# Sums in another form, casts and a table load behind the output's cast, and more output buffers, in a fused attention and mixture-of-experts kernel

## The chip, the cores and the metric

The kernel runs on one core of a Trainium2 chip. The metric is the device time of one execution in microseconds; before the change it is 619.33 us, the median of three runs (619.21 to 619.78). Five engines of the core work side by side: PE (TensorE, matrix products), DVE (VectorE), ACT (ScalarE), POOL (GpSimd) and SP (SyncE, which issues DMAs). Each runs its own queue of instructions in order and waits for others by semaphores.

## The reference

For 4 batches and 8 heads, with 576 positions of 64 numbers each, the attention computes

```python
scores = scale * q @ k.T          # causal mask
a = exp(scores - max); a /= a.sum(-1) + 1e-09
local = a @ v
q_p = phi(q)                      # x + 1 for x > 0, else exp(x)
mem_out = (q_p @ M_prev) / (q_p @ z_prev + 1e-06)
g = sigmoid(beta)                 # one number a head
attn = g * mem_out + (1 - g) * local
```

and its output, 2304 tokens of 512 numbers, goes through `(silu(x @ w_gate) * (x @ w_val)) @ w_out` with 1536 hidden units. All numbers are float32.

## The kernel before

The 32 heads are worked on as 16 pairs, `n` = 0 to 15. The loop over `n` (L543) is a pipeline of two pairs: iteration n computes the scores of pair n and the weighted values of pair n-1 (`old`), and splits the queries and keys of pair n+1; n=16 only drains. Products keep float32 precision by splitting each operand into a high and a low part (`qh`, `ql`, `kh`, `kl`, `xh`, `xl`) and adding three products.

For one pair: PE makes the scores tile by tile (`s`), DVE reads each from PSUM, masks it and takes the row's extreme (`mx`; the tiles `ps`, `pl` and, for the last 64 rows of both heads, `p`), ACT takes the exponential and the row's sum (`sm`), and POOL scales the row by the reciprocal of that sum, `rs`, times the gate `og` = 1 - g (function `weighed`, L436). `weighed` is called three times an iteration: for the four tiles of the first 256 rows, the four of the next 256, and the last 64 rows; the sum `sm + 1e-9` and its reciprocal stand on DVE, first with 128x4 numbers, again with 128x4, and then with 128x1. In an iteration of n=1 or more the first of these stands between `w` (the memory's normaliser) and `mem`, and behind `mem` come the readings of the next scores. The third stands right behind `ph`, DVE's part of phi, a `scalar_tensor_tensor` of 128x640 on two SBUF tiles. POOL's other work in an iteration is the splitting of pair n+1 (`kh`, `qh` early, `ql`, `kl` later).

PE transposes the scaled rows, ACT and DVE copy them to `g1` and `g2`, and PE multiplies them with the values into `tr`. `leave` (L517) casts this output: ACT makes `xh` (128x256 and then, at the next iteration's start, 128x320), DVE `xl`, and SP stores both to DRAM.

Four thirds of the experts' weights are decoded beside the attention (`EARLY`, n = 2, 6, 10, 14): the bits of two halves are put together by DVE (`wa`), and ACT casts the high part (`wgh`, `woh`) in `third_word` (L219), called at the end of n=5, 9 and 13. So the cast lies on ACT between the two `xh` casts. At n=16 ACT loads the table for Silu through a call on a 128x1 tile (`warm`, L553).

`gates` (L143) makes the gates once, in n=0. The order of instructions on PE, ACT, DVE and POOL is the order in the program: the helper `queued` (L79) ties each to the one before, and so nearly all rows carry L84. Exceptions are the DMAs and the cast of `kh` for pair 1, which a scheduler places. The second half of the kernel, from about 189 us on, is the mixture of experts; its output leaves through `away` (L782), with three `pt` buffers.

Of the kernel before, what the change touches and what calls it, by code (L numbers as in the profile page):

```python
# [9 lines left out]
F32 = mybir.dt.float32  # L10
# [3 lines left out]
AF = mybir.ActivationFunctionType  # L14
ALU = mybir.AluOpType
# [6 lines left out]
NP = B * NPAIR  # L22
# [7 lines left out]
ORDER = (0, 768, 1536)  # L30
EARLY, AHEAD = (2, 6, 10, 14), (1, 5, 9, 11, 12, 13, 14)
PLAIN = 3
ACT_K = (0, 1)
# [7 lines left out]
W_ONE = 2.0**-8  # L41
# [3 lines left out]
def attention_moe(ctx: ExitStack, tc: tile.TileContext, qt, kt_, v, m, beta, wg, wv, wo, out):  # L45
    nc = tc.nc
    PE, ACT, DVE, POOL, SP = nc.tensor, nc.scalar, nc.vector, nc.gpsimd, nc.sync

    const = ctx.enter_context(tc.tile_pool(name="const", bufs=1))
# [45 lines left out]
    def rot(pool, name, shape, dtype, n):  # L95
        held = slots.setdefault(name, [0, []])
        if len(held[1]) < n:
            held[1].append(pool.tile(shape, dtype, name=f"{name}{len(held[1])}"))
        held[0] += 1
        return held[1][(held[0] - 1) % n]  # L100
# [14 lines left out]
    warm = const.tile([128, 1], F32, name="warm")  # L115
# [18 lines left out]

    gt = const.tile([128, 8], F32, name="gt")
    gx = const.tile([128, NPAIR, 5, 2], F32, name="gx")

# [3 lines left out]
    def gates():  # L143
        act.activation(gs, gt, AF.Exp)
        act.activation(gt, gt, AF.Exp, scale=-1.0)
        gp, sp = (x.rearrange("p (r j) -> p r j", j=2) for x in (gt, gs))

        def one_less():
            dve.tensor_scalar(gs, gs, 1.0, None, op0=ALU.add)
            dve.reciprocal(gs, gs)  # L150
            dve.tensor_copy(og[:, :, 0:2], sp)
            for j in range(2):
                rows = slice(j * 64, j * 64 + 64)
                dve.tensor_copy(og[rows, :, 2], sp[rows, :, j])

        def memory():
            dve.tensor_scalar(gt, gt, 1.0, None, op0=ALU.add)
            dve.tensor_copy(gx, gp.unsqueeze(2).to_broadcast([128, NPAIR, 5, 2]))

        return one_less, memory  # L160
# [55 lines left out]
        else:  # L216
            act.activation(wa[n], last_byte, AF.Identity, scale=1.0 / 32, bias=low_bias)

    def third_word(act, dve, n):  # L219
        f, j = thirds[n]  # L220
        a, top = wa.pop(n), tops.pop(n).bitcast(I32)
        dve.scalar_tensor_tensor(
            out=a, in0=top, scalar=3, in1=a, op0=ALU.logical_shift_left, op1=ALU.bitwise_or
        )
        raws.pop(n)
        c = slice(j * 512, j * 512 + 512)
        if j < 2:
            SP.dma_start(wdr[f, :, c], a.bitcast(F32))
            if f >= PLAIN:
                return  # L230
            if j == 0:
                held[f] = [rot(wp, f"wg{part}", [128, 1024], F32R, 2) for part in "hl"]
            oh, ol = (x[:, c] for x in held[f])
        else:
            wout[f] = oh, ol = [rot(wp, f"wo{part}", [128, 512], F32R, 3) for part in "hl"]
        act.copy(oh, a.bitcast(F32))
        low_parts.append((f, j, a.bitcast(F32), oh, ol))

    def third(n):
# [9 lines left out]
    with tc.tile_pool(name="sb", bufs=1, reuse_waits="tile") as sb:  # L249
# [24 lines left out]
        def pair_split(n, raw):  # L274
            qr, kr = raw
            q = [rot(sb, f"q{part}", [128, 640], F32R, NK) for part in "hl"]
            k = [rot(sb, f"k{part}", [128, 576], F32R, NK) for part in "hl"]
            if n == 0:
                cuts = [(slice(0, 256), slice(0, 256)), (slice(256, 576), slice(256, 640))]
                lo = lambda dst, src, hi: dve.tensor_tensor(dst, src, hi.bitcast(F32), op=ALU.subtract)  # L280
                raw = qr[:, 128:768]
                for ck, cq in cuts:
                    act.copy(k[0][:, ck], kr[:, ck])
                    split_hi(q[0][:, cq], raw[:, cq])
                (ck, cq), (dk, dq) = cuts
                lo(k[1][:, ck], kr[:, ck], k[0][:, ck])
                lo(q[1][:, cq], raw[:, cq], q[0][:, cq])
                lo(k[1][:, dk], kr[:, dk], k[0][:, dk])
                return q, k, lambda: lo(q[1][:, dq], raw[:, dq], q[0][:, dq])
            (ACT.copy if n in ACT_K else split_hi)(k[0], kr)  # L290
            split_hi(q[0], qr[:, 128:768])

            def lows():
                split_lo(q[1], qr[:, 128:768], q[0], "q")
                split_lo(k[1], kr, k[0], "k")

            return q, k, lows
# [21 lines left out]
        class Pair:  # L319
# [58 lines left out]
            def scores(self, t):  # L378

                w = 128 * (t + 1)  # L380
                ps = [rot(psS, "s", [128, 512], F32, PS_S) for _ in range(2)]
                for i, (q, k) in enumerate(self.products):
                    for h in range(2):
                        rows = slice(h * 64, h * 64 + 64)
                        mm = pe.matmul(
                            ps[h][:, 0:w], q[rows, t * 128 : t * 128 + 128], k[rows, 0:w], start=(i == 0), stop=(i == 2)
                        )
                        if i == h == 0 and id(ps[1]) in read:
                            follow(mm, read[id(ps[1])], "once both banks are read", mybir.DependencyClass.Sync)

                def reading(h):
                    p = rot(sb, "pl", [128, 512], F32, NBIG) if t > 1 else rot(sb, "ps", [128, 256], F32, NSMALL)
                    read[id(ps[h])] = dve.tensor_tensor_reduce(
                        out=p[:, 0:w], in0=ps[h][:, 0:w], in1=maskp[:, 512 - w : 512], op0=ALU.add, op1=ALU.min,
                        scale=-SCALE, scalar=BIG, accum_out=self.mx[:, 2 * t + h : 2 * t + h + 1],
                    )
                    self.pts[(t, h)] = p

                return reading

            def exp(self, t, h):
                c, p = 2 * t + h, self.pts[(t, h)][:, 0 : 128 * (t + 1)]
                act.activation(
                    p, p, AF.Exp, bias=self.mx[:, c : c + 1], scale=-1.0, accum_out=self.sm[:, c : c + 1]
                )
# [27 lines left out]
                p = self.pts[(4, 0)][:, 0:576]  # L433
                act.activation(p, p, AF.Exp, bias=self.mx[:, 9:10], scale=-1.0, accum_out=self.sm[:, 8:9])

            def weighed(self, keys):  # L436

                c, n = keys[0][0] * 2, len(keys)
                rs = rot(sb, "rs", [128, 5], F32, 6)[:, 0:n]
                dve.tensor_scalar(rs, self.sm[:, c : c + n], 1.0e-9, None, op0=ALU.add)  # L440
                dve.reciprocal(rs, rs)
                for i, (t, h) in enumerate(keys):
                    p = self.pts[(t, h)][:, 0 : min(576, t * 128 + 128)]
                    g = h if t < 4 else 2
                    pool.tensor_scalar(
                        p, p, rs[:, i : i + 1], og[:, self.pr, g : g + 1], op0=ALU.mult, op1=ALU.mult
                    )

            def recalled(self):

# [89 lines left out]
        phi0 = pairs[0].phi_parts()  # L540
        nothing = lambda *args: None
        ending = lambda: nothing
        for n in range(NP + 1):  # L543
            cur = pairs[n] if n < NP else None
            old = pairs[n - 1] if n > 0 else None
# [3 lines left out]
            turned, turned1 = (old.turned, old.turned1) if old else (nothing, nothing)  # L549
            if cur:  # L550
                cur.begin()
            if n == NP:
                act.activation(warm, warm, AF.Silu)  # L553
            if old:
                old.turns()
            low = ending()
            reads = [scores(t) for t in range(2)]
            reads[0](0)
            reads[0](1)
# [15 lines left out]
            turned(2, 0, dve)  # L575
            turned(2, 1, dve)
            if n == NP:
                for i in range(2):
                    raw_top(act, len(EARLY) + i)
                third_clamp(pool, len(EARLY))  # L580
                third_move(pool, len(EARLY))
# [14 lines left out]
            reads = [scores(t) for t in range(2, 4)]  # L596
            reads[0](0)
            reads[0](1)
            exp(2, 0)
            exp(2, 1)  # L600
            turned(3, 0, act)
# [6 lines left out]
            exp(3, 1)  # L608
            if n == 0:
                one_less()  # L610
                first()
            read4()
            if cur:
                cur.exp4()
# [25 lines left out]
            for i, at in enumerate(EARLY):  # L640
                if n == at:
                    raw_top(act, i)
                if n == at + 1:
                    third_clamp(dve, i)
                if n == at + (2 if i < 3 else 1):
                    third_move(dve, i)
                if n == at + 3 and i < 3:
                    third_word(act, dve, i)
                if n == at + 4 and i < 3:
                    low_part(dve)  # L650
            if n in AHEAD:
# [10 lines left out]
    with tc.tile_pool(name="stg2", bufs=1, reuse_waits="tile") as stg2, \  # L662
# [117 lines left out]
                leave.append(lambda: away(t0, j))  # L780

        def away(t0, j):  # L782
            pt = rot(mbp, "pt", [128, 512], F32, 3)
            if t0 == ORDER[-1] and j % 2:
                dve.tensor_scalar(pt, po[j], W_ONE, None, op0=ALU.mult)
            else:
                act.mul(pt, po[j], W_ONE)
            SP.dma_start(out[t0 + j * 128 : t0 + j * 128 + 128, :], pt)

        hold = lambda name, k=2: rot(near if name in ("zg", "zh") else mbp, name, [128, N2], F32, k)  # L790
        halves_due = []
# [221 lines left out]
```

## Time and profile before

| | |
|---|---|
| median of three runs | 619.33 us (619.21 to 619.78) |
| the profiled execution | 619.71 us |
| its span (first to last instruction) | 617.9 us |
| PE busy | 602.4 us (97%) |
| DVE busy | 486.1 us (79%) |
| ACT busy | 394.5 us (64%) |
| POOL busy | 217.1 us (35%) |
| DMA | 102.46 MB, mean 166 GB/s |

Busy shares are averages over two unlike halves: most of POOL's 217 us lie in the first 190 us. A row of a timeline gives the start, the time to the end, the engine, the line, the operation and the tiles; what is in brackets behind it is how long the engine was idle before and what released it. An instruction's time includes what it stands inside the engine, for instance for a path to the memory that another engine holds; only waits for semaphores are told as idle.

### The profile page before, as it was taken

To read this page: it belongs to the slowest core of one execution; us is meant where nothing else is said; L and a number is where in the kernel's file an instruction comes from. 1 tells how busy PE (TensorE), PEld (TensorE's weight loads), DVE (VectorE), ACT (ScalarE), POOL (GpSimd) and SP (SyncE) were. 2 spreads that over 40 slices of the span, in tenths; PEclk is the share of its full clock that TensorE was granted. 3 is DMA by queue.
4 is the path that set the end of the run, shared out by engine and by line. 5 is a ranking of instruction groups with operands and counts; after the bars stand their busy time and mean duration, and the time that the engine had idled before them with its cause. 6 is when DMAs were issued, how large, how long until landed. Compare 5 with 4: busy or idle time off the path is not lost.

```text
span 617.9 us, 11275 instructions
## 1 busy us (share of the span) xinstructions
PE 602.4 (97%) x3794; PEld 535.6 (87%) x3794; DVE 486.1 (79%) x1210; ACT 394.5 (64%) x914; POOL 217.1 (35%) x261
## 2 busy tenths in 40 slices
PE   5999999999999999999999999999999999999997
PEld 4777788778778999999899999999999999999995
DVE  7999999899987978888998765665898765665653
ACT  7787888888885678777667654454456654454442
POOL 6999999999964344433420000000000000000000
PEclk9999999999999999999999999999999999999999
DMA  8455856657328657799646631323754621322202
GB/s 247 121 167 153 274 159 195 229 167 221 140 83 286 194 172 231 234 342 293 212 153 221 207 101 69 104 101 112 231 184 172 208 100 68 108 99 68 75 29 102
DMA packets 49177, 102.46 MB, mean 166 GB/s; under 512 B 7008, under 2 KB 16864, under 8 KB 49120
## 3 DMA queue, kind: packets, MB, share of 16 engines
q1 hardware_dynamic: 48832, 101.45, 50.4%
q8 instruction: 30, 0.49, 0.3%
q10 hardware_dynamic: 288, 0.30, 0.1%
q14 instruction: 27, 0.22, 0.1%
HBM read 74.99 MB, written 26.74 MB: 165 GB/s over the span
## 4 chain that ended last, share of the span: by engine, by line
PE 91%; DVE 5%; ACT 2%; issue 1%; DMA 1%; DVEq 0%; ACTq 0%
PE s L84 58%; PE tr L84 33%; ACT pl L84 1%; DVE rs L84 1%; DVE mem L84 1%; DVE pl L84 1%; DVE xl L84 1%; DMA kr<-in_kt_dram 0%; ACT g L84 0%; DVE w L84 0%; DVE ph L84 0%; DMA out_dram<-pt 0%; DVE wa L84 0%; ACT xh L84 0%; DVE gs L84 0%
## 5 line engine op out<-in xcount | busy, mean ns | idle before, releaser
L84 ACT ACTIVATE zh<-zh 128x384 f32<-128x384 f32 x33 | 17.4, 528 | 75.9 <-DVE zh L84 75.9
L84 POOL TENSOR_SCALAR pl<-pl,rs,og 128x384 f32<-128x384 f32 (+1 forms) x64 | 56.7, 897 | 10.1 <-DVE rs L84 10.1
L84 DVE TENSOR_TENSOR zv<-s,zv 128x384 f32<-128x384 f32 x33 | 18.4, 557 | 52.4 <-PE s L84 47.2
L84 PE MATMUL tr<-woh,uh 128*128 128x512 f32 x144 | 57.1, 397 | 0.0
L84 PE MATMUL tr<-woh,ul 128*128 128x512 f32 x144 | 56.8, 394 | 0.0
L84 PE MATMUL tr<-wol,uh 128*128 128x512 f32 x144 | 56.5, 392 | 0.0
L84 POOL TENSOR_SCALAR we<-we 128x512 f32<-128x512 f32 x32 | 27.7, 867 | 76.0 <-ACT we L84 75.8
L84 ACT ACTIVATE pl<-pl,mx 128x384 f32<-128x384 f32 (+1 forms) x64 | 42.3, 663 | 14.6 <-DVE mx L84 14.6
L84 PE MATMUL tr<-g,vp 128*64 128x320 f32 (+4 forms) x448 | 48.7, 360 | 0.0
L84 DVE TENSOR_TENSOR tl<-tt,th 128x512 fp32r<-128x512 f32 x66 | 47.6, 721 | 0.0
L84 ACT CAST th<-tt 128x512 fp32r<-128x512 f32 x66 | 41.1, 622 | 8.2 <-DVE tt L84 4.6
L84 PEld LDWEIGHTS tr<-g,vp 128*64 128x64 f32 x448 | 29.4, 137 | 17.6 <-issue 2.5
L84 PE MATMUL s<-kh,qh 64*128 64x128 f32 (+4 forms) x160 | 37.5, 388 | 7.2 <-ACT kh L84 4.2
L84 DVE TENSOR_TENSOR zg<-s,zp 128x384 f32<-128x384 f32 x33 | 18.4, 558 | 28.2 <-ACT bh L84 21.1
L84 DVE CUSTOM_DVE_ANT_0 pl<-s,maskp 128x384 f32<-128x384 f32 (+1 forms) x64 | 38.1, 616 | 0.7 <-PE s L84 0.7
L84 ACT CAST uh<-zh 128x384 fp32r<-128x384 f32 x36 | 18.5, 514 | 31.4 <-DVE zh L84 31.1
L84 DVE TENSOR_TENSOR bl<-wr,bh 128x512 fp32r<-128x512 f32 x66 | 36.3, 550 | 0.0
L84 PE MATMUL tr<-ident,pl 128*128 128x128 f32 x224 | 31.9, 280 | 2.7 <-DVE xl L84 2.7
L84 ACT CAST bh<-wr 128x512 fp32r<-128x512 f32 x66 | 33.9, 513 | 0.0
L84 DVE COPY g<-tr 128x384 f32<-128x384 f32 (+1 forms) x64 | 32.0, 519 | 1.6 <-PE tr L84 0.2
L84 PEld LDWEIGHTS tr<-woh,ul 128*128 128x128 f32 x144 | 27.0, 188 | 7.1 <-DVE ul L84 0.3
L84 PEld LDWEIGHTS tr<-ident,pl 128*128 128x128 f32 x224 | 25.3, 143 | 9.0 <-POOL pl L84 3.5
(190 smaller groups left out, 2004.4 us busy)
## 6 DMA issues: line engine op xcount, KB each, us to landing
wr<-wdr SPq DMA_DIRECT2D x24, 512.0 KB, 3.3
wraw<-in_wg_dram SPq DMA_DIRECT2D x12, 512.0 KB, 4.5
wraw<-in_wv_dram SPq DMA_DIRECT2D x12, 512.0 KB, 5.1
wraw<-in_wo_dram SPq DMA_DIRECT2D x12, 512.0 KB, 5.1
wol<-wdo SPq DMA_DIRECT2D x24, 256.0 KB, 2.8
woh<-wdo SPq DMA_DIRECT2D x24, 256.0 KB, 3.2
qr<-in_qt_dram SPq DMA_DIRECT2D x15, 384.0 KB, 3.1
vp<-in_v_dram SPq DMA_DIRECT2D x16, 320.0 KB, 4.5
```

Source lines behind the costliest of these rows:

```text
L84: ins = getattr(eng, name)(*args, **kw)
```

## The change

- `rs`: the sum `sm + 1e-9` is a `tensor_tensor` with a constant tile `tiny` (all 1e-9), no longer a `tensor_scalar` with an immediate. `gs + 1` and `gt + 1` likewise, with a tile `ones`.
- `one_less`: three reciprocals write `og`, in place of one reciprocal and three copies.
- n=0: the first `rs` and its reciprocal stand ahead of the readings of the fourth scores; the scaling on POOL stands where it stood, behind `one_less`. The cast of `kh` for pair 1 stands in ACT's program order, behind the exponentials of `ps`.
- The casts of `third_word` in the attention are put into a list, `copies`, and issued behind the second `xh` cast of the next iteration. The Silu call at n=16 stands behind `xh` and two copies `g`.
- `away`: six `pt` buffers; the last tile is scaled in two halves, by ACT and by DVE, and stored by the DMA queues of ACT and SP.

```diff
+    tiny = const.tile([128, 5], F32, name="tiny")
+    DVE.memset(tiny, 1.0e-9)
+    ones = const.tile([128, 8], F32, name="ones")
+    DVE.memset(ones, 1.0)
...
         def one_less():
-            dve.tensor_scalar(gs, gs, 1.0, None, op0=ALU.add)
-            dve.reciprocal(gs, gs)
-            dve.tensor_copy(og[:, :, 0:2], sp)
+            dve.tensor_tensor(gs, gs, ones, op=ALU.add)
+            dve.reciprocal(og[:, :, 0:2], sp)
             for j in range(2):
                 rows = slice(j * 64, j * 64 + 64)
-                dve.tensor_copy(og[rows, :, 2], sp[rows, :, j])
+                dve.reciprocal(og[rows, :, 2], sp[rows, :, j])
...
-        act.copy(oh, a.bitcast(F32))
+        if later is None:
+            act.copy(oh, a.bitcast(F32))
+        else:
+            later.append(lambda: act.copy(oh, a.bitcast(F32)))
...
-            (ACT.copy if n in ACT_K else split_hi)(k[0], kr)
+            (act.copy if n in ACT_K else split_hi)(k[0], kr)
...
-            def weighed(self, keys):
+            def normal(self, keys):
...
-                dve.tensor_scalar(rs, self.sm[:, c : c + n], 1.0e-9, None, op0=ALU.add)
+                dve.tensor_tensor(rs, self.sm[:, c : c + n], tiny[:, 0:n], op=ALU.add)
                 dve.reciprocal(rs, rs)
...
-            if n == NP:
-                act.activation(warm, warm, AF.Silu)
             if old:
                 old.turns()
             low = ending()
+            while copies:
+                copies.pop(0)()
...
             turned(2, 1, dve)
             if n == NP:
+                act.activation(warm, warm, AF.Silu)
...
+            if n == 0:
+                scaled = cur.normal(((0, 0), (0, 1), (1, 0), (1, 1)))
             exp(2, 0)
...
             if n == 0:
                 one_less()
-                first()
+                scaled()
...
-            pt = rot(mbp, "pt", [128, 512], F32, 3)
+            pt = rot(mbp, "pt", [128, 512], F32, 6)
+            rows = slice(t0 + j * 128, t0 + j * 128 + 128)
+            if t0 == ORDER[-1] and j == TURN[-1]:
+                act.mul(pt[:, 0:256], po[j][:, 0:256], W_ONE)
+                ACT.dma_start(out[rows, 0:256], pt[:, 0:256])
+                dve.tensor_scalar(pt[:, 256:512], po[j][:, 256:512], W_ONE, None, op0=ALU.mult)
+                SP.dma_start(out[rows, 256:512], pt[:, 256:512])
+                return
```

DVE in n=0, before: `pl` and `p` are readings of scores (ISA rows, with the row that stores `mx` behind each), then the gate and `rs`.

```order
L84 ISA pl_214,mx_147<-s_157,maskp 128x512
L84 ISA mx_147 128x1
L84 ISA pl_216,mx_147<-s_158,maskp 128x512
L84 ISA mx_147 128x1
L84 TENSOR_SCALAR gs<-gs 128x8
L84 RECIPROCAL gs<-gs 128x8
L84 COPY og<-gs 128x4x2
L84 COPY og<-gs 64x4 x2
L84 TENSOR_SCALAR rs_225<-sm_148 128x4
L84 RECIPROCAL rs_225<-rs_225 128x4
L84 ISA p_206,mx_147<-s_149,maskp 128x288
L84 ISA mx_147 128x1
```

The same place after: `rs` and its reciprocal stand ahead of the last two readings of `pl`.

```order
L84 TENSOR_TENSOR rs_208<-sm_152,tiny 128x4
L84 RECIPROCAL rs_208<-rs_208 128x4
L84 ISA pl_221,mx_151<-s_161,maskp 128x512
L84 ISA mx_151 128x1
L84 ISA pl_223,mx_151<-s_162,maskp 128x512
L84 ISA mx_151 128x1
L84 TENSOR_TENSOR gs<-gs,ones 128x8
L84 RECIPROCAL og<-gs 128x4x2
L84 RECIPROCAL og<-gs 64x4 x2
L84 ISA p_213,mx_151<-s_153,maskp 128x288
L84 ISA mx_151 128x1
L84 ISA p_213,mx_151<-s_154,mask_91,mx_151 128x288
```

The pair of `rs` went ahead of four rows and of `gs`; behind `gs` there are three instructions for four.

ACT at the start of n=6, before: the two `xh` casts of pair 5's output, the weight's cast, and the first exponential of pair 6.

```order
L84 ACTIVATE p_358,sm_251<-p_358,mx_250 128x576
L84 CAST xh_415<-tr_296 128x256
L84 CAST wgh_1011<-wa_864 128x512
L84 CAST xh_415<-tr_301 128x320
L84 ACTIVATE ps_165,sm_148<-ps_165,mx_147 128x128
```

The same place after.

```order
L84 ACTIVATE p_361,sm_254<-p_361,mx_253 128x576
L84 CAST xh_418<-tr_299 128x256
L84 CAST xh_418<-tr_304 128x320
L84 CAST wgh_1014<-wa_867 128x512
L84 ACTIVATE ps_169,sm_152<-ps_169,mx_151 128x128
```

The weight's cast went behind the second `xh`; what follows is as it was. At n=10 it is the same, and at n=14 with `woh`.

ACT at n=16, before: the table load and the call on `warm` stand between the two `xh` casts of pair 15.

```order
L84 CAST xh_415<-tr_296 128x256
L84 ACT_TABLE_LOAD
L84 ACTIVATE warm<-warm 128x1
L84 CAST xh_415<-tr_301 128x320
L84 COPY g_252<-tr_284 128x384
L84 COPY g_252<-tr_289 128x384
L84 ACTIVATE we_1160<-wraw_422 128x512
```

The same place after.

```order
L84 CAST xh_418<-tr_299 128x256
L84 CAST xh_418<-tr_304 128x320
L84 COPY g_255<-tr_287 128x384
L84 COPY g_255<-tr_292 128x384
L84 ACT_TABLE_LOAD
L84 ACTIVATE warm<-warm 128x1
L84 ACTIVATE we_1163<-wraw_425 128x512
```

The load and the call went behind the second `xh` and the two copies `g`, and stand right ahead of `we`, the preparation of the next weights.

## Rows read from the trace of the kernel before

**Rows 1.** The chain that ended last (part 4 of the page), share of the span by engine.

```profile
PE 91%; DVE 5%; ACT 2%; issue 1%; DMA 1%; DVEq 0%; ACTq 0%
```

**Rows 2.** What PE waited for, 0 to 200 us: total, times, longest.

```profile
PE s L84 <- DVE mx L84: 2.9, 4, 1.7
...
PE tr L84 <- DVE xl L84: 2.7, 4, 1.0
```

**Rows 3.** Iterations by stretches: length, busy time (instructions) by engine, PEclk, DMA share, GB/s.

```profile
49.24:60.63 11.39, 11.13 (x105) 8.87 (x101) 10.62 (x40) 9.20 (x26) 10.44 (x14) 1.00 0.55 153
60.63:71.38 10.75, 10.75 (x106) 8.81 (x103) 10.02 (x40) 9.25 (x26) 10.34 (x14) 1.00 0.77 247
...
115.80:127.60 11.80, 11.21 (x105) 8.85 (x101) 10.59 (x41) 9.88 (x28) 10.83 (x14) 1.00 0.53 179
...
sum 145.20, PE 143.09 PEld 115.09 DVE 134.31 ACT 122.22 POOL 137.07; mean PE 11.01 PEld 8.85 DVE 10.33 ACT 9.40 POOL 10.54
```

**Rows 4.** Timeline of DVE at n=4, n=5: start us, us, engine, line, op, out<-in, xcount.

```profile
53.20 0.76 DVE L84 TENSOR_SCALAR rs<-sm 128x4 f32<-128x4 f32 x1
...
64.60 0.11 DVE L84 TENSOR_SCALAR rs<-sm 128x4 f32<-128x4 f32 x1
```

**Rows 5.** Timeline of POOL at n=4.

```profile
53.21 0.73 POOL L84 TENSOR_SCALAR qh<-qr 128x640 fp32r<-128x640 f32 x1
```

**Rows 6.** Timeline of ACT and PE at the start of n=10; idle before in brackets.

```profile
116.86 0.63 ACT L84 CAST wgh<-wa 128x512 fp32r<-128x512 f32 x1 [1.43 <-DVE wa L84]
...
117.39 0.41 ACT L84 CAST xh<-tr 128x320 fp32r<-128x320 f32 x1
...
118.47 0.30 PE L84 MATMUL tr<-ident,pl 128*128 128x128 f32 x1 [0.59 <-DVE xl L84]
```

**Rows 7.** Timeline of DVE, small sums: n=1, and behind ph at n=8.

```profile
16.53 0.16 DVE L84 TENSOR_SCALAR gt<-gt 128x8 f32<-128x8 f32 x1
...
104.65 0.15 DVE L84 TENSOR_SCALAR rs<-sm 128x1 f32<-128x1 f32 x1
```

**Rows 8.** Timeline of DVE, large instructions with two SBUF inputs.

```profile
4.13 0.42 DVE L84 TENSOR_TENSOR kl<-kr,kh 128x256 fp32r<-128x256 f32 x1 [2.13 <-ACT kh L84]
...
4.47 0.73 DVE L84 TENSOR_TENSOR ql<-qr,qh 128x256 fp32r<-128x256 f32 x1
...
199.61 1.36 DVE L84 TENSOR_TENSOR xr<-xp1h,xp1l 128x768 f32<-128x768 f32 x1
```

**Rows 9.** Timeline of POOL beside them.

```profile
4.42 0.51 POOL L84 TENSOR_SCALAR qh<-qr 128x384 fp32r<-128x384 f32 x1 [0.37 <-DMA qr<-in_qt_dram]
...
15.90 1.35 POOL L84 TENSOR_SCALAR pl<-pl,rs,og 128x512 f32<-128x512 f32 x1
...
104.20 1.07 POOL L84 TENSOR_SCALAR pl<-pl,rs,og 128x384 f32<-128x384 f32 x1 [0.41 <-DVE rs L84]
...
199.20 0.96 POOL L84 TENSOR_SCALAR we<-we 128x512 f32<-128x512 f32 x1
```

**Rows 10.** Timeline of DVE, POOL and PE at n=0.

```profile
10.03 1.41 POOL L84 TENSOR_TENSOR kl<-kr,kh 128x576 fp32r<-128x576 f32 x1
...
10.40 1.06 DVE L84 TENSOR_SCALAR gs<-gs 128x8 f32<-128x8 f32 x1
...
13.62 0.58 PE L84 MATMUL s<-kh,qh 64*128 64x256 f32 x2 [1.69 <-DVE mx L84]
```

**Rows 11.** Timeline of DVE and PE at n=16.

```profile
183.48 0.41 DVE L84 TENSOR_SCALAR wa<-wraw 128x512 int32<-128x512 int32 x1
...
184.33 0.49 DVE L84 TENSOR_TENSOR xl<-tr,xh 128x320 fp32r<-128x320 f32 x1 [0.45 <-ACT xh L84]
...
184.97 0.30 PE L84 MATMUL tr<-ident,pl 128*128 128x128 f32 x1 [0.98 <-DVE xl L84]
```

**Rows 12.** Timeline of PE and ACT at the end.

```profile
613.02 0.40 PE L84 MATMUL tr<-woh,ul 128*128 128x512 f32 x1
...
614.19 0.60 ACT L84 ACTIVATE pt<-tr 128x512 f32<-128x512 f32 x1 [0.74 <-DMA out_dram<-pt]
```

More of the change, by code (lines that the diff above doesn't have):

```diff
@@ L148, in one_less @@
         def one_less():
-            dve.tensor_scalar(gs, gs, 1.0, None, op0=ALU.add)
-            dve.reciprocal(gs, gs)
-            dve.tensor_copy(og[:, :, 0:2], sp)
+            dve.tensor_tensor(gs, gs, ones, op=ALU.add)
+            dve.reciprocal(og[:, :, 0:2], sp)
             for j in range(2):
                 rows = slice(j * 64, j * 64 + 64)
-                dve.tensor_copy(og[rows, :, 2], sp[rows, :, j])
+                dve.reciprocal(og[rows, :, 2], sp[rows, :, j])
         def memory():
-            dve.tensor_scalar(gt, gt, 1.0, None, op0=ALU.add)
+            dve.tensor_tensor(gt, gt, ones, op=ALU.add)
             dve.tensor_copy(gx, gp.unsqueeze(2).to_broadcast([128, NPAIR, 5, 2]))
@@ L217, in third_move, with third_word @@
             act.activation(wa[n], last_byte, AF.Identity, scale=1.0 / 32, bias=low_bias)
-    def third_word(act, dve, n):
+    def third_word(act, dve, n, later=None):
         f, j = thirds[n]
@@ L434, in exp4, with scaled, weighed @@
                 act.activation(p, p, AF.Exp, bias=self.mx[:, 9:10], scale=-1.0, accum_out=self.sm[:, 8:9])
-            def weighed(self, keys):
+            def normal(self, keys):
                 c, n = keys[0][0] * 2, len(keys)
                 rs = rot(sb, "rs", [128, 5], F32, 6)[:, 0:n]
-                dve.tensor_scalar(rs, self.sm[:, c : c + n], 1.0e-9, None, op0=ALU.add)
+                dve.tensor_tensor(rs, self.sm[:, c : c + n], tiny[:, 0:n], op=ALU.add)
                 dve.reciprocal(rs, rs)
[L442 to L447, printed above, removed]
+                def scaled():
+                    for i, (t, h) in enumerate(keys):
+                        p = self.pts[(t, h)][:, 0 : min(576, t * 128 + 128)]
+                        g = h if t < 4 else 2
+                        pool.tensor_scalar(
+                            p, p, rs[:, i : i + 1], og[:, self.pr, g : g + 1], op0=ALU.mult, op1=ALU.mult
+                        )
+                return scaled
+            def weighed(self, keys):
+                self.normal(keys)()
             def recalled(self):
@@ L542, in attention_moe @@
         ending = lambda: nothing
+        copies = []
         for n in range(NP + 1):
@@ L647, in attention_moe @@
                 if n == at + 3 and i < 3:
-                    third_word(act, dve, i)
+                    third_word(act, dve, i, copies)
                 if n == at + 4 and i < 3:
@@ L787, in away @@
                 act.mul(pt, po[j], W_ONE)
-            SP.dma_start(out[t0 + j * 128 : t0 + j * 128 + 128, :], pt)
+            SP.dma_start(out[rows, :], pt)
         hold = lambda name, k=2: rot(near if name in ("zg", "zh") else mbp, name, [128, N2], F32, k)
```

## The prediction

> **What bounds the kernel now.** I read the chain that ended last first, then PE's waits, then the attention cut by iteration. 91% of the chain lies on PE [rows 1], so in the second half (the mixture of experts) nothing is to be had but the very end. In the first 200 us PE waits 2.9 us for `mx`, which is VectorE's reading of the scores, and 2.7 us for `xl`, the low half of the attention's output [rows 2]. Cut at the first scores product of each pair, the thirteen whole iterations n=2 to n=14 take 145.20 us together; PE works through 143.09 of them, but POOL is busy for 137.07, a mean of 10.54 out of 11.17, and the mean of VectorE is 10.33 [rows 3]. So these iterations are a loop that turns at the pace of three engines. Their lengths are unlike: 10.75, 11.39 and 11.80 stand there [rows 3].
>
> The difference hangs on one small instruction. In each iteration VectorE's sum `rs <- sm` (128x4, adding 1e-9) is followed by a reciprocal, the two `mem` products, and then the reading of scores on which PE waits. At n=4 that sum took 0.76 us, at n=5 only 0.11 [rows 4]; 11.39 - 0.76 = 10.63 and 10.75 - 0.11 = 10.64, so the iteration is 10.64 plus the length of this sum. A sum of 512 numbers is no work of 0.76 us: at n=4 it went from 53.20 to 53.96, and POOL's `qh` from 53.21 to 53.94 [rows 4, 5]. VectorE's sum stood until POOL's instruction was through. The third kind of iteration, n=6, 10 and 14, costs up to 11.80: there ScalarE casts a weight (0.63 us) ahead of the output's `xh`, `xl` comes late and PE stands for 0.59 [rows 6].
>
> **The sums in two-tensor form.** The change turns 48 sums `rs`, and `gs` and `gt`, from one tensor and an immediate into two tensors, both in SBUF. The trace of before has no small instruction of that form, so I bound it from both sides. If the form doesn't stand behind POOL, it costs what small ones cost that met no hindrance, 0.11 to 0.16 [rows 4, 7]. If it does, it costs what the old form cost, and what remains is the question whom it hits. The nearest rows are VectorE's large two-tensor instructions: `kl` 128x256 took 0.42, and `ql`, of the same size and kind, 0.73 while POOL's second `qh` ran from 4.42 to 4.93 beside it, so that its last 0.27 fell behind POOL's end [rows 8, 9]. I therefore take it that the new form stands as the old one did, and that `rs` of 128x4 gains nothing by itself. The Trainium skill says the same (SBUF — State Buffer, "Who interferes with whom"): a VectorE instruction with two inputs in SBUF contends with a GpSimd instruction that reads SBUF, and the one that comes second waits for the whole of the other. `ql` agrees with it. By that rule the change of form is worth nothing, and it adds contenders.
>
> For sixteen of the sums are `rs` of 128x1, and these did not stand in the old form: at n=8 it took 0.15 from 104.65, while POOL's first `pl` was under way from 104.20 for 1.07 us [rows 7, 9]. In the new form they can stand. What happens there depends on who is let through when `ph` ends: `ph` has two SBUF inputs and itself held up that `pl`, and VectorE's sum comes right behind it. The nearest case in rows is `gt` behind `ph`: it took 0.16 from 16.53 while POOL's `pl` of 15.90 stretched to 1.35, so VectorE kept its place [rows 7, 9]. Against it, `xr` came right behind another two-tensor instruction of VectorE at 199.61, and yet POOL's `we`, on its row since 199.20, went first and was through at 200.16; `xr` ended 0.81 later [rows 8, 9]. I take `gt`, since it is small, behind the same `ph`, and against the same `pl`. Then the price is on POOL: its `pl` starts later by the gap and the sum, about 0.1 an iteration. The ends are 0, and 0.5 us of VectorE's time: from 104.65 to the end of that `pl` at 105.27 are 0.62, less the sum's own 0.15.
>
> **The casts behind `xh`.** Three times (n=6, 10, 14). `xh` of 128x320 can then start about when the weight's cast did, at 116.86 instead of 117.39, 0.53 earlier [rows 6]. `xl` is next held by VectorE's own order (weight word and two readings of scores), and PE's 0.59 shrinks to nearly nothing. But POOL was busy 10.83 in such an iteration [rows 3] and stands idle another 0.41 for `rs` at its `pl` [rows 9], so 11.24 is its floor: 11.80 - 11.24 gives 0.55 each, 1.65 together. Moved along is one weight DMA at each place on SP's queue (`wdr` twice, `wdo` once), now behind that of `xh`; nothing near reads what they write, and `xh`'s own goes earlier. The exponentials stood behind both casts before and do so now. With `pl` 0.1 later in each iteration, the ten plain ones would give back up to 1.0; but the sums of n=3 and 4, which stood longest, meet POOL elsewhere. I take +0.25 for the ten. Sum of the loop: -1.4, and its ends -4.0 and +3.3 are the rivals'.
>
> **The start.** VectorE's `gs` sum went from 10.40 for 1.06 us, and POOL's `kl` until 11.44 beside it; PE then stood 1.69 until 13.62 [rows 10]. After the change `rs` and its reciprocal are done earlier, among readings for which VectorE waits on PE anyway, and three reciprocals write `og` in place of one reciprocal and three copies. `rs` would itself stand there for POOL's `ql`, which is hidden as far as `gs` must wait for `kl` all the same. What is saved is the two `rs` instructions (0.35) and the one less (about 0.15): 0.5. If the later phase lets the first sum of n=1 catch an earlier end on POOL, another 0.9 goes. I take 0.9; the ends are 0.3 and, if no sum stands, 2.4. The two memsets at the start stand where VectorE has nothing to do yet.
>
> **The table load.** At n=16 it stands ahead of `xh`, and PE waited 0.98 for `xl` until 184.97 [rows 11]. With the load behind `xh`, `xl` is held by VectorE's `wa`, 183.48 to 183.89 [rows 11]; it would start at 183.9 instead of 184.33. Gain 0.4, with ends 0.2 and 0.9: the load now lies ahead of the preparation of the next weights, which had about 0.3 to spare.
>
> **The end.** The last matmul ends at 613.42, but the last `pt` starts at 614.19, since it waited for a buffer that a DMA was still reading [rows 12]. It ends at 614.79, and the span 3.1 later. With six buffers nothing waits; the two halves start at 613.45 and 613.5 and, of half the size, end by 613.9. Gain 0.9, with ends 0.7 and 1.2, since each half has its own queue and the path of 3.1 stays.
>
> **The sum.** -1.4 - 0.9 - 0.4 - 0.9 = -3.6. The profiled execution took 619.71, 0.38 above the median 619.33 of the three runs; 616.1 on its scale is 615.7 on that of the median. The likeliest case's own range is 614.3 to 617.0.
>
> **Rivals.** (A) The change does as its words suggest and the new form doesn't stand at all. For it: 128x1 sums never stood, so form decides. Against it: `ql`, a two-tensor instruction that did. Then a sum takes about 0.16, each iteration 10.80 by VectorE and some 10.84 by POOL, and the thirteen come to 141.2 with a little left of the casts: -4.0. With -2.4 at the start, -0.5 and -0.9: -7.8, or 611.5.
>
> (B) The sum of 128x1 behind `ph` stands for POOL's `pl`, 0.5 us in each iteration. Then `xl` and the first readings of scores are late by that, and the `rs` of 128x4 behind them misses the end of POOL's `kh` and waits for that of `qh` (53.94 in the rows, as at n=4, the slow kind [rows 5]). Eight iterations of 11.34 (10.64 plus some 0.70) and five of 11.56 come to 148.5, +3.3. With -0.9 at the end, -0.3 at the table load and -0.9 at the start, +1.2: 620.5. It decides from about 0.35 us of standing. By the words of the Trainium skill in the same section, that the order of issue decides, POOL's `pl`, issued before the sum, would go first, which is this case; `gt` speaks against it and `xr` for it.
>
> (C) It stands in some iterations and not in others, since POOL's phase differs from one to the next: between, 617.5 to 619.5.
>
> **How the numbers follow.** Forecast 0.43, A 0.16, B 0.25, C 0.11, and 0.05 for a new wait that I don't see and that makes it slower. About 0.2% or 1.24 us is what a measurement of this kernel tells from no change; the bounds are 618.1 and 620.6. Faster: forecast, A, and a third of C, 0.63. B lies astride the upper bound: 0.12 of it within, 0.13 above; with the rest of C and the new wait: same 0.19, slower 0.18. The likeliest case's own range misses too much, so it reaches from A to B, 611.0 to 620.9.
>
> **What would show it.** Right: `rs` of 128x4 still ends with an instruction of POOL; `rs` of 128x1 takes about 0.15; PE's wait for `xl` goes from 2.7 to under 0.7; n=6, 10, 14 take about 11.2; the last `pt` starts by 613.5 on the old scale. A: every `rs` takes 0.16, PE's wait for `mx` is nearly gone. B: `rs` of 128x1 takes 0.5 or more, and plain iterations 11.3. Wrong altogether: iterations over 11.6, or PE waiting for a weight behind n=16.

## The result

The changed kernel takes 612.64 us (median of four runs, 612.23 to 613.29), the one before 619.27 in the runs beside it; the ratio is 0.9894, with a 95% interval of 0.9876 to 0.9911. That is 6.6 us faster, inside the forecast range of 611.0 to 620.9 but 3.1 us below the forecast of 615.7 and below the likeliest case's own range (614.3 to 617.0). The profiled execution took 612.91 us, its span 611.1 against 617.9. Between the two profiled executions the 6.8 us of span go as follows (cut at the starts of the first scores product of a pair and of VectorE's `zv`, which stands once in each unit of the experts):

| stretch | before | after | change | forecast |
|---|---|---|---|---|
| start, to the first product of n=2 | 26.85 | 26.10 | -0.75 | -0.9 |
| iterations n=2 to n=14 | 145.20 | 143.43 | -1.77 | -1.4 |
| n=15 to the first `zv` of the experts | 61.60 | 60.89 | -0.71 | -0.4 |
| first to last `zv`, 32 units | 371.19 | 368.40 | -2.79 | 0 |
| last `zv` to the end of the span | 13.10 | 12.31 | -0.79 | -0.9 |

Four terms came out near their forecast, though for the start and the loop that is in part chance (see the account below). The largest part of the gain was not in the forecast at all: the experts, which the change doesn't touch, go 0.087 us faster in each of 32 units.

### The profile page after: what moved, and what is told of

The parts are those of the page before. It is cut to its first block, busy times and chain, and to the rows that moved or that the text cites. A ratio compares the mean times of both kernels' runs of the same rounds, so it can differ in the third digit from the quotient of the medians.

```text
span 611.1 us, 11285 instructions
## 1 busy us (share of the span) xinstructions
PE 599.4 (98%) x3794; PEld 531.1 (87%) x3794; DVE 486.5 (80%) x1212; ACT 395.0 (65%) x914; POOL 217.0 (36%) x261
## 4 chain that ended last, share of the span: by engine, by line
PE 94%; DVE 3%; ACT 1%; issue 1%; DMA 0%; DVEq 0%
PE s L84 59%; PE tr L84 35%; DVE rs L84 1%; DVE pl L84 1%; DMA kr<-in_kt_dram 0%; ACT pl L84 0%; DVE mem L84 0%; ACT g L84 0%; DVE w L84 0%; DVE ps L84 0%; DVE p L84 0%; DVE xl L84 0%; DVE ql L84 0%; DVE g L84 0%; ACT ps L84 0%
## 5 line engine op out<-in xcount | busy, mean ns | idle before, releaser
L84 ACT ACTIVATE ps<-ps,mx 128x128 f32<-128x128 f32 (+1 forms) x64 | 28.6, 453 | 6.3 <-DVE mx L84 6.3
```

The lines of the kernel that those rows point to most:

```text
L84: ins = getattr(eng, name)(*args, **kw)
```

## The profile after

What PE waited for in the first 200 us, changed kernel (total, times, longest), against [rows 2]:

```profile
PE s L84 <- DVE mx L84: 1.5, 3, 1.1
PE s L84 <- DVE gs L84: 0.7, 1, 0.7
PE tr L84 <- DVE xl L84: 0.4, 1, 0.4
PE tr L84 <- ACT g L84: 0.4, 1, 0.4
```

The wait for `xl` went from 2.7 to 0.4, as the casts' and the table load's steps say. That for `mx` went from 2.9 to 1.5; the difference lies in n=1, where 1.69 became 1.06 and another 0.83 went. New is the 0.7 for `gs`, ahead of the first product of n=1. The iterations (columns as in [rows 3]), n=4, 5, 10 and the sum of n=2 to 14:

```profile
48.50:59.88 11.38, 11.13 (x106) 8.88 (x102) 10.60 (x40) 9.21 (x26) 10.45 (x14) 1.00 0.54 153
59.88:70.63 10.75, 10.75 (x106) 8.80 (x103) 10.03 (x40) 9.25 (x26) 10.34 (x14) 1.00 0.77 246
...
114.51:125.62 11.11, 11.11 (x105) 8.81 (x101) 10.40 (x41) 9.99 (x28) 10.70 (x14) 1.00 0.54 171
...
sum 143.43, PE 143.00 PEld 114.96 DVE 134.16 ACT 122.53 POOL 137.09; mean PE 11.00 PEld 8.84 DVE 10.32 ACT 9.43 POOL 10.55
```

n=4 and n=5 are what they were (11.39 and 10.75), and n=10 lost 0.69 of its 11.80. The sums, on VectorE's timeline, at n=4, at n=8 behind `ph`, and at n=15, where there is no `ph`:

```profile
52.47 0.74 DVE L84 TENSOR_TENSOR rs<-sm,tiny 128x4 f32<-128x4 f32 x1
...
103.39 0.15 DVE L84 TENSOR_TENSOR rs<-sm,tiny 128x1 f32<-128x1 f32 x1
...
179.84 0.39 DVE L84 TENSOR_TENSOR rs<-sm,tiny 128x1 f32<-128x1 f32 x1 [0.47 <-ACT p L84]
```

and POOL beside them:

```profile
52.48 0.73 POOL L84 TENSOR_SCALAR qh<-qr 128x640 fp32r<-128x640 f32 x1
...
102.94 1.07 POOL L84 TENSOR_SCALAR pl<-pl,rs,og 128x384 f32<-128x384 f32 x1 [0.41 <-DVE rs L84]
...
179.57 3.21 POOL L84 TENSOR_SCALAR pl<-pl,rs,og 128x384 f32<-128x384 f32 x4 [3.51 <-DVE rs L84]
```

These answer [rows 4, 5, 7, 9]. The two-tensor sum of 128x4 stands behind POOL's `qh` exactly as the old form did, 52.47 to 53.21 both. The sum of 128x1 right behind `ph` takes 0.15, and keeps its place although `pl` has been on POOL's row since 102.94. At n=15 VectorE comes from idle, `pl` has been running since 179.57, and now the small sum does stand, 0.39, until that first `pl` ends. In the kernel before, the same sum at the same place, with `pl` running since 181.98, did not:

```profile
182.25 0.15 DVE L84 TENSOR_SCALAR rs<-sm 128x1 f32<-128x1 f32 x1 [0.47 <-ACT p L84]
```

The sum of pair 0, which falls into n=1 and comes right behind a reading of scores, stood too, 0.60 beside `pl`; in the old form (experiment 3) the same sum took 0.15:

```profile
14.59 0.60 DVE L84 TENSOR_TENSOR rs<-sm,tiny 128x1 f32<-128x1 f32 x1
```

```profile
14.47 0.15 DVE L84 TENSOR_SCALAR rs<-sm 128x1 f32<-128x1 f32 x1
```

So the new form contends in 128x1 too: the two sums that don't stand right behind `ph` were held up, and the fourteen that do were spared.

The cast place, start of n=10 (ACT, DVE), against [rows 6]:

```profile
114.62 0.43 ACT L84 CAST xh<-tr 128x320 fp32r<-128x320 f32 x1 [0.48 <-PE tr L84]
...
114.84 0.70 DVE L84 SCALAR_TENSOR_TENSOR wa<-we,wa 128x512 int32<-128x512 int32 x1
...
115.58 0.62 ACT L84 CAST wgh<-wa 128x512 fp32r<-128x512 f32 x1 [0.53 <-DVE wa L84]
...
115.89 0.48 DVE L84 TENSOR_TENSOR xl<-tr,xh 128x320 fp32r<-128x320 f32 x1
```

`xh` now runs before the weight's cast, and `xl` follows VectorE's own order; PE waits for it no more. At n=16 (against [rows 11]) and at the end (against [rows 12]):

```profile
181.40 0.48 DVE L84 TENSOR_TENSOR xl<-tr,xh 128x320 fp32r<-128x320 f32 x1
...
182.03 0.52 PE L84 MATMUL tr<-ident,pl 128*128 128x128 f32 x3 [0.43 <-DVE xl L84]
...
607.00 0.39 PE L84 MATMUL tr<-woh,ul 128*128 128x512 f32 x1
607.42 0.38 ACT L84 ACTIVATE pt<-tr 128x256 f32<-128x256 f32 x1 [0.80 <-PE tr L84]
...
607.84 0.42 DVE L84 TENSOR_SCALAR pt<-tr 128x256 f32<-128x256 f32 x1 [0.42 <-ACT pt L84]
```

PE's wait fell from 0.98 to 0.43. At the end no `pt` waits for a DMA; but DVE's half was released by ACT's (the bracket), 0.4 later than the forecast had it: the two halves of one tile went one after the other.

The experts, 30 units from the second `zv` on, before and after (columns as in [rows 3]):

```profile
245.19:593.26 348.07, 348.07 (x1802) 322.93 (x1801) 257.62 (x478) 193.82 (x393) 27.59 (x24) 1.00 0.47 157
```

```profile
241.83:587.34 345.51, 345.51 (x1802) 319.41 (x1801) 257.67 (x478) 193.83 (x393) 27.36 (x24) 1.00 0.48 158
```

PE is busy throughout in both, at the same clock and with the same number of products; DVE, ACT and DMA did the same work. The products themselves follow one another faster. Two kinds of them, 245 to 590 us, in the kernel before (count, busy us, mean ns):

```profile
L84 PE MATMUL s<-xp7l,th 128*128 128x384 f32 x58 | 19.7, 339 | 0.0
...
L84 PE MATMUL s<-xp7h,tl 128*128 128x384 f32 x58 | 19.6, 339 | 0.0
```

and after:

```profile
L84 PE MATMUL s<-xp7h,tl 128*128 128x384 f32 x60 | 20.1, 336 | 0.0
...
L84 PE MATMUL s<-xp7l,th 128*128 128x384 f32 x60 | 20.1, 334 | 0.0
```

A product overlaps the next one and its end is modelled, so the distance from its start to the next start is the safer measure: a mean of 177.8 ns before and 172.8 after for `xp7l,th`, 177.6 and 173.8 for `xp7h,tl`. Not all kinds gain: `tr<-woh,ul` went from 231.2 to 235.8.

## The experiments

Two questions were open: why the experts go faster, and whether the attention's terms have the causes that were given. The suspect for the first was the place of tiles: `tiny` and `ones` take 64 bytes in each partition, so all tiles allocated behind them, with the weights' `th`, `tl`, `bh`, `bl` that TensorE holds stationary, lie 64 bytes further; the inputs `x` and the `pt` buffers lie on the other side of the memory, and six `pt` move some of them by 6144. "A unit" below is the mean of the 32 distances between the 33 `zv` rows: 11.600 us before, 11.513 after (the expectations of 1 and 2 have their median, 11.57 and 11.48). The kernel before took 619.76 (median) beside the first four, 619.34 beside the next four and 619.36 beside the last four.

**1. The kernel before, with the space alone.**

```diff
+    tiny = const.tile([128, 5], F32, name="tiny")
+    DVE.memset(tiny, 1.0e-9)
+    ones = const.tile([128, 8], F32, name="ones")
+    DVE.memset(ones, 1.0)
```

> The kernel before, with the two constant tiles allocated and filled but used by nothing. All tiles allocated behind them (the weights, their high and low parts, the attention's tiles) lie 64 bytes further in each partition; no other instruction changes. Theory P, that the place of the tiles sets the pitch of the expert products: a unit of the experts takes 11.48 us instead of 11.57 and the time falls by 2.9, to about 616.4; the attention stays at 10.84 to 11.80 an iteration. Rival R, that the faster experts come from an edit of the change (buffers, order, what the attention leaves behind): a unit stays at 11.57 and the time at 619.3.

617.32 us, ratio 0.996 (0.9946 to 0.9973). A unit 11.513; the attention's loop (n=2 to n=14) 145.19 against 145.20. Thirty units:

```profile
244.85:590.38 345.53, 345.53 (x1802) 319.37 (x1801) 257.62 (x478) 193.59 (x393) 27.36 (x24) 1.00 0.47 158
```

Two constants that nothing reads make the experts as fast as they are in the changed kernel. Theory P holds.

**2. The changed kernel, with the tiles where they were.**

```diff
-    warm = const.tile([128, 1], F32, name="warm")
+    pad = const.tile([128, 8], F32, name="warm")
+    warm, tiny = pad[:, 0:1], pad[:, 1:6]
...
+    ones = one.to_broadcast([128, 8])    # one: a free column of low_bias
```

> The changed kernel, with its constants kept in unused columns of tiles that were there already, so that the weights' tiles lie where they lay before. Theory P: a unit of the experts goes back to 11.57, the time rises by 2.9 to about 615.5, which is the sum that was predicted. Rival R: a unit stays at 11.48 and the time at 612.6.

615.85 us, ratio 0.9938 (0.9925 to 0.995). A unit 11.600, the loop 143.26. Without the moved tiles the change gives 3.9 us, where 3.6 were forecast. The two runs also divide the stretch from n=15 to the first `zv`, which holds some products of the experts: 61.32 in experiment 1 and 61.15 here, against 61.60, so 0.28 of its 0.71 comes with the tiles' place and 0.45 with the change.

**3. The sums in their old form, no tile moved.**

```diff
-                dve.tensor_tensor(rs, self.sm[:, c : c + n], tiny[:, 0:n], op=ALU.add)
+                dve.tensor_scalar(rs, self.sm[:, c : c + n], 1.0e-9, None, op0=ALU.add)
```

(and `gs`, `gt` likewise)

> The changed kernel, with the sums rs, gs and gt again as tensor and immediate; the constant tiles stay, unused, so that no tile moves. Theory of the prediction (both forms stand behind POOL's instruction, so the form is worth nothing): 612.6, within 0.5 either way, and rs of 128x4 ends with POOL's instructions as before. Rival A (the two-tensor form doesn't stand): the time rises by 2 us or more.

612.96 us, ratio 0.9889 (0.9876 to 0.9903), against 0.9894 (0.9876 to 0.9911) of the changed kernel: the form is worth nothing that these runs can tell. The sums of 128x4 stand in this form too: at n=3 0.67 us, against 0.68 in the changed kernel. One detail differs. At n=4 the sum slipped in ahead of POOL's `qh`:

```profile
52.32 0.11 DVE L84 TENSOR_SCALAR rs<-sm 128x4 f32<-128x4 f32 x1
```

```profile
52.33 0.73 POOL L84 TENSOR_SCALAR qh<-qr 128x640 fp32r<-128x640 f32 x1
```

and that iteration took 10.74 instead of 11.38. It was close: in the changed kernel, where the sum stood, the two rows start 0.01 apart as well (52.47 and 52.48), so the rows don't show what decided. n=5 was caught by `qh` in experiments 4, 6 and 8 (11.38, 11.37, 11.37) and not in the other runs that have the sum.

**4. Three `pt` buffers again.**

```diff
-            pt = rot(mbp, "pt", [128, 512], F32, 6)
+            pt = rot(mbp, "pt", [128, 512], F32, 3)
```

> The changed kernel with three pt buffers again; the last tile still leaves in two halves. The tiles on the right side of the memory lie where they lay before. Prediction's term for the end: the last pt waits for its buffer again, its halves start 0.7 later, and the time rises by 0.5 to 0.9 to about 613.3. If the experts' pitch came from the right side's tiles (a rival to the left side's in theory P): a unit back at 11.57 and 615.5 or more.

614.76 us (612.6 to 615.47), ratio 0.9912 (0.9897 to 0.9927). A unit stays at 11.513, so the right side's 6144 bytes are not the cause. From the last `zv` to the end of the span 13.08 instead of 12.31: the term of the end, 0.77. The rest of the difference between the two profiled executions lies before: the loop (0.48, n=5 above all), and a start of 27.38 instead of 26.10, in which the clock stayed at half for longer. 17 to 19 and 19 to 21 us, here and in the changed kernel (the column ahead of the last two is the granted clock):

```profile
17.00:19.00 2.00, 2.00 (x10) 1.86 (x9) 1.32 (x4) 1.45 (x5) 2.00 (x4) 0.50 0.22 86
19.00:21.00 2.00, 2.00 (x11) 1.78 (x12) 1.24 (x6) 0.74 (x1) 0.83 (x3) 0.50 0.03 8
```

```profile
17.00:19.00 2.00, 2.00 (x16) 1.88 (x17) 1.28 (x4) 1.96 (x6) 2.00 (x4) 0.86 0.35 138
19.00:21.00 2.00, 1.96 (x19) 1.32 (x15) 1.92 (x9) 0.32 (x2) 1.55 (x4) 1.00 0.03 8
```

Why the low stretch (1.2 GHz instead of 2.4) is longer here stays open. The number of buffers is an unlikely cause, since the first `pt` is written at 337 us, but one profiled execution of each kernel doesn't show it.

**5. No sum at all.** The row sum is at least 1, so adding 1e-9 changes no bit of it in float32.

```diff
-                dve.tensor_tensor(rs, self.sm[:, c : c + n], tiny[:, 0:n], op=ALU.add)
-                dve.reciprocal(rs, rs)
+                dve.reciprocal(rs, self.sm[:, c : c + n])
```

> The changed kernel with the sum of rs left out: the reciprocal reads sm itself. The row sum is at least 1, since the largest term is exp(0), and 1e-9 is below its last place. No tile moves. Theory of the prediction: the 128x4 sums stood behind POOL, so the iterations that they lengthened (n=2, 3, 4, 7, 11 with 11.09 to 11.38) come down to about 10.85, together -1.6, and the time to about 611.2; in the others POOL's own 10.4 and its wait remain, and nothing goes. Rival (the length of the sum only mirrors another wait, which takes its place): 612.8.

608.4 us, ratio 0.9824 (0.9809 to 0.9839): as fast as any kernel here, and much better than the expected 611.2. The loop:

```profile
25.02:164.39 139.37, 139.36 (x1318) 114.53 (x1315) 128.56 (x469) 123.60 (x345) 138.42 (x170) 1.00 0.62 197
```

143.43 became 139.37, and PE is busy without a gap. Plain iterations take 10.65 to 10.66, those with casts 10.78 to 10.85; one plain iteration, n=4, took 11.05, where VectorE stood idle 0.68 ahead of its second `w` (0.28 at n=5), so not every long iteration is a sum's. The expectation of 10.85 by POOL was wrong; the other rule, 10.64 plus the sum's length, held in the other plain iterations, with a sum of nothing. In the changed kernel the thirteen first sums are 3.9 us together, near the 4.06 that went. But n=6, 10 and 14 lost 0.27 to 0.33 with first sums of 0.12: there the rule falls short, and no run shows what went besides. The reciprocal of 128x4 itself did not stand: 0.12 to 0.18 in all of them.

**6. The casts ahead again.**

```diff
-                    third_word(act, dve, i, copies)
+                    third_word(act, dve, i)
```

> The changed kernel with the weights' casts ahead of the output's second cast again. Prediction's term: n=6, 10, 14 go back to 11.8 with PE's wait of 0.59 for xl, the three iterations behind them fall from 11.1 to 10.97, together +1.6, and the time rises to about 614.4. Rival (POOL alone sets these iterations): within 0.3 of 612.8.

615.5 us (614.12 to 615.82), ratio 0.9931 (0.9913 to 0.995). n=6, 10 and 14 took 11.64, 11.80 and 11.80, n=7 and 11 behind them 10.95 and 10.94, and the wait is back:

```profile
PE tr L84 <- DVE xl L84: 2.1, 4, 0.6
```

The loop took 145.63, 2.20 more than in the changed kernel, of which 0.62 is n=5's sum (experiment 3): 1.6 for the casts, as expected. The time is 1.1 above the expected 614.4; in the profiled execution the start is 0.81 longer as well, though nothing up to n=2 differs.

**7 to 12. Which place it is.** All are made from the changed kernel; in 9 to 12 the sums of `rs` are left out, which doesn't touch the experts. Spare tiles move the left side (weights), the right side (inputs), or only the experts' operand tiles:

```diff
+    space = const.tile([128, 8], F32, name="space")     # 7: 32 bytes, tiny and ones as in 2
+    space = const.tile([128, 88], F32, name="space")    # 8: the left side at 416
+    far = edge.tile([128, 120], F32, name="far")        # 8: the right side lower by 480
+    far = edge.tile([128, 16], F32, name="far")         # 9: by 64; the left side as in 2
+    space = const.tile([128, 8], F32, name="space")     # 10: the left side at 96
+    space = const.tile([128, 16], F32, name="space")    # 11: at 128
+    space = stg2.tile([128, 16], F32, name="space")     # 12: tt, th, tl, bh, bl alone, by 64
```

Experiment 7:

> The changed kernel, with the tiles on the left side 32 bytes further than before instead of 64 (the weights' tiles at 128 in a line of 512 bytes; 96 before, 160 after). Theory P in the form that only distance counts: a unit of the experts between 11.513 and 11.600. In the form that lines of 64 or 128 bytes count: at 11.513 or below, since the tiles then begin on such a line.

Experiment 8:

> The changed kernel, with spare space so that the weights' tiles on the left and the inputs' tiles on the right (480 in a line of 512 before and after) all begin on a line of 512 bytes. If alignment of each tile counts: a unit of the experts well below 11.513, and the time below 612. If the distance between the two tiles that TensorE reads counts, no better than 11.513.

Experiment 9:

> The kernel without the sums of rs, with the left side's tiles where they lay before (weights at 96 in a line of 512 bytes) and the right side's 64 bytes lower (inputs at 416 instead of 480), so that the distance between the two is that of the changed kernel. If the distance of the tiles that TensorE reads together sets the pitch: a unit of the experts 11.513, time 608.4. If the weights' own place does: 11.600 and 611.3.

Experiment 10:

> The kernel without the sums of rs, the left side's tiles 96 bytes further than in the kernel before (weights at 192 in a line of 512). No theory gives a number here; so far 0, 32 and 64 bytes gave 11.600, 11.624 and 11.513. If the pitch is good on multiples of 64 past 96, it is about 11.62; the attention is untouched, and the time is 608.4 plus 33 times the difference to 11.513.

Experiment 11:

> As the last one, 128 bytes further (weights at 224 in a line of 512). If the pattern has a period of 128 bytes: 11.600 and 611.3, as at 0. Otherwise a value of its own; a value below 11.513 would be a faster kernel than any so far.

Experiment 12:

> The kernel without the sums of rs, the left side's tiles where they lay before, but for the experts' operand tiles (tt, th, tl, bh, bl), 64 bytes further. If the place of TensorE's stationary operands sets the pitch: a unit of 11.513 and 608.4. If it is that of the moving weights of the last product (woh, wol, which stay) or of the attention's tiles: 11.600 and 611.3.

"Weights" and "inputs" are the places of `th` and its fellows and of the `x` tiles in a line of 512 bytes, "distance" the first less the second in it (512 is chosen for the table; no run shows that it is a period).

| kernel | weights | inputs | distance | a unit, us | time, us |
|---|---|---|---|---|---|
| before, 2 | 96 | 480 | 128 | 11.600 | 619.3, 615.85 |
| 7 | 128 | 480 | 160 | 11.624 | 616.03 |
| after, 1, 3 to 6 | 160 | 480 | 192 | 11.513 | 612.64 (after) |
| 10 | 192 | 480 | 224 | 11.564 | 610.18 |
| 11 | 224 | 480 | 256 | 11.625 | 611.74 |
| 8 | 0 | 0 | 0 | 11.626 | 616.04 |
| 9 | 96 | 416 | 192 | 11.513 | 607.87 |
| 12 (`woh`, `wol` at 96) | 160 | 480 | 192 | 11.496 | 608.19 |

Experiment 9 tells most. Its weights lie where they lay before and its inputs 64 bytes lower, and the unit is 11.513:

```profile
236.44:581.96 345.52, 345.52 (x1802) 319.47 (x1801) 257.68 (x479) 193.71 (x393) 27.33 (x24) 1.00 0.47 158
```

That the unit is the same could be chance; the kinds of product settle it. From start to next start, each of the 27 kinds in these units comes to the same mean within 0.5 ns here and in the changed kernel, while the kernel before and the changed one differ by up to 5.0 ns. So it is the distance between the two sides that counts, and not where either lies. Experiments 8 and 11, at distances of 0 and 256, agree in all kinds within 0.5 ns too, so as far as two kernels tell, the pattern repeats after 256 bytes. Experiment 12 narrows it to `tt`, `th`, `tl`, `bh` and `bl`: the attention's tiles and `woh` stay, and the unit is as short, even 0.017 shorter. Not everything goes by a product's own two tiles: those of `woh` and `wol`, 128 apart as before, took 232.4, 230.9 and 232.1 ns there (`woh,uh`, `wol,uh`, `woh,ul`), against 235.3, 229.9 and 231.2 in the kernel before. VectorE and ScalarE read and write the moved tiles as well; no run separates this from TensorE's own reading, and why the distance counts stays open. Aligning everything on 512 (8) is the slowest of all, with 7 and 11 close to it. Times of 7 to 12 are single runs and the last column is no ranking; the unit is a mean over 32.

## Why the prediction was right, and where not

The number lies within the range by its width: the range reached down to rival A, and 612.64 is nearer to A's 611.5 than to the forecast, though A's mechanism didn't come about. Most of the argument for the attention held:

- *The form of the sums*: forecast to be worth nothing by itself; experiment 3 shows it for the time. Rival A fell with the first row of 128x4 that ended with `qh`.
- *Sixteen new contenders*: taken to keep their place behind `ph`, and the fourteen of n=1 to n=14 did, at 0.15; that of n=15, without `ph` ahead, stood for 0.39 as in rival B, and so did pair 0's in n=1, for 0.60. The price of 0.1 an iteration on POOL isn't there: at n=8 its `pl` takes 1.07 and starts 0.45 ahead of the sum, as before. The +0.25 for the ten plain iterations came to +0.32 for another reason: n=7 and n=11, behind the casts, took 0.16 and 0.14 longer, the others the same within 0.03.
- *The casts*: 1.65 forecast for the three iterations; they lost 2.09, of which n=7 and n=11 gave back 0.31. Experiment 6 shows 1.6 for the sum of these.
- *The table load*: 0.4 forecast, PE's wait fell by 0.55, and 0.45 went of the stretch in experiment 2; no run takes this edit back by itself.
- *The end*: 0.9 forecast, 0.79 between the profiles and 0.77 in experiment 4; the second half's time was wrong by 0.4, since the halves don't overlap.
- *The start*: 0.9 forecast, 0.75 between the profiles, but three kernels that are the same up to n=2 reached it at 26.10, 27.38 and 26.91 (changed, experiments 4 and 6), so its size is not settled, and no run takes its edits back. It didn't come as forecast either: the first `rs` stood 1.29 us beside POOL's `ql` (from 8.77), which was not hidden, for n=1 began at 11.62 instead of 10.63 (at 10.64 in experiment 4, where that `rs` took 0.16); what was gained lies in n=1 itself, 14.48 instead of 16.21.

Two steps failed. The first is the sentence "so in the second half (the mixture of experts) nothing is to be had but the very end": it read a PE that is busy without a gap as a PE that can't go faster. 2.8 of the 6.8 us came from there. What the runs show in its place is that the products' own pace depends on where the tiles lie. Experiments 1 and 2 show it from both sides, 2.4 us (619.76 to 617.32) and 2.9 us (615.85 against the 612.96 of experiment 3, which differs but in the sums' form); without it the kernel is at 615.85, against the forecast of 615.7. The diff did show the two new tiles; what was missing was the question of what they move.

The second is POOL's floor, "11.24 is its floor", and 10.84 for plain iterations in rival A. The three iterations took 11.05 to 11.12 after the change and 10.78 to 10.85 without sums, and plain ones 10.65. POOL's 10.4 to 10.8 of busy time held its own standing for VectorE (1.07 us for a `pl` that overlaps `ph`), so busy time plus idle time was no bound: without sums POOL is busy for 138.42 us of the loop instead of 137.09, with the same 170 instructions, in a loop 4.06 shorter. The error was small in the forecast, but in experiment 5 it hid 2.5 us of the gain.

## What to carry to other kernels

Before a gain or loss is put down to an edit, see what the edit did to the place of the tiles: a run of the old kernel with nothing but the new space tells it. Where a stretch is all TensorE, a few spare bytes that shift the stationary operands against the streamed ones are worth a scan; here 11.50 to 11.63 us a unit. A small instruction that stands behind another engine is better removed than rewritten, and the busy time of the engine that it stands behind is not all work: it holds that engine's own standing.

## What was new of the hardware

- Products of the same shape at the same clock followed one another after 172.8 or 177.8 ns (`xp7l,th`) by where the tiles of the two sides of the memory lay to each other; a distance of 192 against 128 is worth 0.75% of the experts' time.
- A two-tensor sum of 128x4 and one of tensor and immediate both ended with POOL's running instruction (0.74 us at n=4, 0.67 at n=3); a reciprocal of the same size never did (0.12 to 0.18).
- VectorE's next instruction right behind one for which POOL stood kept its place (0.15 behind `ph`, fourteen times); the same one out of idle stood (0.39), and so did one behind a reading of scores (0.60).
